# Windowed attention and a gated convolutional feed-forward on one core: batch 0 loaded and attended in two token halves

## The chip, the cores and the metric

The kernel runs on one core of a Trainium2 chip, as one program. The metric is the device time in microseconds (us) of that core. A core has a matrix engine (TensorE, PE in the profile; PEld is its loading of weights), VectorE (DVE), ScalarE (ACT), GpSimd (POOL), and SyncE (SP), whose queue here issues nearly all DMA transfers. The engines run beside each other, each in its own fixed order, and wait for one another through semaphores. PE writes to PSUM, which has eight banks; only DVE and ACT move results from there to SBUF in this kernel.

## The reference: what is computed

There are 8 batches of 576 tokens, 8 heads of 64. Each token attends to the tokens at most 32 places away. The heads are then put side by side (512 numbers per token) and go through a feed-forward with 1024 inner channels and a gate from a convolution over three neighbouring tokens.

```python
scores = scale * np.matmul(q, k.transpose(0, 1, 3, 2))
mask = np.abs(pos[:, None] - pos[None, :]) <= 32
attn = exp(where(mask, scores, -1e9) - max); attn /= attn.sum(-1)
x = np.matmul(attn, v).transpose(0, 2, 1, 3).reshape(B, S, H * D)
h = np.maximum(x @ w_in, 0.0)                      # (B, S, 1024)
conv = sum(conv_w[k] * hp[:, k:k + S, :] for k in range(3))
out = (h * sigmoid(conv)) @ w_out                  # (B, S, 512)
```

## The kernel before

**Attention of one batch.** Heads are taken in four pairs. `loads` (line 349) brings q and k in by four transfers of 576 KB (two for q, two for k: `load_qk`), and v in five blocks of up to 128 tokens (`load_v`); POOL casts each to bf16 (`cast_qk`, `cast_v`). v is cast into `ve`, and DVE copies it shifted by 64 tokens into `vo` (`shift`), so that each window finds its tokens on the right partitions. `transposes` (line 475) turns q and k on PE into `qT` and `kT`, through PSUM and a copy on ACT or DVE. `scores` (line 509) makes the scores of a pair in two pieces (windows 0 to 4 and 5 to 8), ACT takes the exponential into `attn`, and DVE multiplies by the band mask. `values` (line 539) multiplies by v with a column of ones beside it, DVE takes the reciprocal of that sum (`rec`) and scales into `xn`. `x_turned` (line 578) transposes `xn` into `xT`, in groups of two, two and one blocks of 128 tokens.

**Feed-forward.** Two batches are 1152 tokens, cut into three chunks of 384, so there are 12 chunks; chunk 0 lies in batch 0, chunk 1 half in batch 0 and half in batch 1, chunk 2 in batch 1. For a chunk, `first` (line 615) makes eight blocks of 128 inner channels from `w_in_sb` and `xT` (four products each) and a relu on ACT or DVE into `hT`. Chunk 1 is worked in two parts of 193 columns, so that its batch-0 part need not wait for batch 1. `gates` (line 705) does the convolution on PE with 32 x 32 diagonal weights (`diag_w`), four strips of the array at once. A strip's result lands rotated by a multiple of 32 partitions for three of four channel blocks, so `moves` (line 688) copies `hT` rotated into `gT` by DMA; then ACT takes tanh into `tn`, and DVE multiplies (`gT<-tn,hT` for the block that is not rotated, `gT<-tn,gT` for those that were moved). `second` (line 758) multiplies `gT` by `w_out_sb` in three output blocks, which are copied to `wst` and stored.

**Weights.** w_in comes in two halves of 512 columns into the staging tile `ws` (shown as `wst`), cast on POOL (`load_w_in`, line 413); w_out follows into the same tile after batch 1's loads (`load_w_out`, line 429). The stores use that tile, too.

**What sets the order.** No loop of the program order is run as written. Every step is added as a task with the engines that may do it and their assumed durations, its reads and writes, and a target time (`Order.add`, line 39). `Order.run` (line 65) then lists the tasks: of those that are ready on an engine it takes the one with the earliest target, gives out PSUM banks, and where two engines may do a copy takes the one that would end first. The instructions are emitted in the order that comes out and keep it on the chip. The targets come from one table of numbers, `PARAMS` (line 832): the period of the chunks, starts, and an offset for each kind of step. Loads of batch 0 have the target -100, w_in -60, batch 1 -50, w_out -40, so these go in that order on SP. Everything is emitted through one helper, so all rows of the profile name line 274 (line 283 in the changed kernel); steps are told apart by tiles and shapes.

In the shapes, a product of `xT` with `w_in_sb` of 385 or 386 columns is a whole chunk's, one of 193 columns a part of chunk 1. `ident,xn` are the transposes of x; `w_out_sb,gT` with 512 columns the output products.

Of the kernel before, what the change touches and what calls it, by code (L numbers as in the profile page):

```python
# [31 lines left out]
class Order:  # L32
# [3 lines left out]
    def __init__(self):  # L36
        self.tasks, self.writer, self.readers = [], {}, {}

    def add(self, kinds, emit, t, reads=(), writes=(), opens=None, ps=(), after=(), claims=()):


        deps = set(after)
# [10 lines left out]
        task = Task(len(self.tasks), kinds, emit, t, deps, opens, ps)  # L53
        task.soft = soft - deps
        for k in reads:
            self.readers.setdefault(k, []).append(task)
# [138 lines left out]
def kernel(  # L195
# [152 lines left out]

    def loads(b):
        i = b % NLD  # L350

        def load_qk(y, j):
            src = (q, k)[y][b, 4 * j:4 * j + 4, :, :]
            sync.dma_start(
                qkst[y][j].rearrange("p e j d -> p e (j d)"),
                bass.AP(src.tensor, src.offset, [[RP * D, 128], [2 * S * D, 2], [1, RP * D]]),
            )

# [21 lines left out]
        if b < 2:  # L380
            x, dx = (-100.0 if b == 0 else -50.0), 0.1
        else:
            x, dx = t0 - PARAMS["LD"], Q["LX"]
# [5 lines left out]

        for j in range(NPH):  # L390
            for y in range(2):
                t = x + n * dx
                o.add({"SP": dma(256, 110)}, lambda e, y=y, j=j: load_qk(y, j), t,
                      writes=[("st", y, j)], after=paced())
                before.append(o.tasks[-1])
                o.add({"POOL": pl(1152)}, lambda e, y=y, j=j: cast_qk(y, j, e), t,
                      reads=[("st", y, j)], writes=[("b", i, y, j)])
                n += 1
        for c in range(NBLK):
            t = x + n * dx  # L400
            o.add({"SP": dma(1024, 21)}, lambda e, c=c: load_v(c), t, writes=[("vst", c)], after=paced())
            before.append(o.tasks[-1])
            o.add({"POOL": pl(512)}, lambda e, c=c: cast_v(c, e), t,
                  reads=[("vst", c)], writes=[("ve", i, c)])
            n += 1
        for cs in ((0, 2), (2, 4)) if b == 0 else ((0, 4),):
            for half in range(2):
                o.add({"DVE": dve(520 * (cs[1] - cs[0]), 4)},
                      lambda e, cs=cs, half=half: shift(half, cs), x + n * dx,
                      reads=[("ve", i, c + half) for c in range(*cs)],  # L410
                      writes=[("vo", i, c, half) for c in range(*cs)])

    def load_w_in():
        for h in range(2):
# [9 lines left out]
            o.add({"SP": dma(512, 95)}, load, -60.0, writes=[("ws", 4 * h + c) for c in range(4)])  # L424
            for c in range(KC):
                o.add({"POOL": pl(512)}, lambda e, h=h, c=c: cast(e, h, c), -60.0 + h,
                      reads=[("ws", 4 * h + c)], writes=[("w_in", h, c)])

    def load_w_out():
        rows = moe_w_out.rearrange("(h c p) f -> p h c f", c=4, p=128)  # L430
        for c in range(4):
            def load(e, c=c):
                for lo, at, n in turn(c):
# [5 lines left out]
            o.add({"SP": dma(256, 95, len(turn(c)))}, load, -40.0,  # L439
                  writes=[("ws", 4 * h + c) for h in range(2)])  # L440
            for h in range(2):
                o.add({"POOL": pl(512)}, lambda e, h=h, c=c: copy(e, w_out_sb[:, 4 * h + c, :], ws[:, 4 * h + c, :]),
# [18 lines left out]
    def conv_weights():  # L461
        ps = Banks(1)
        o.add({"PE": pe(200.0, "f32")},
              lambda e: tensor.matmul(bank(ps, 0)[:, 0:3 * MB], conv_w24, ident24, start=True, stop=True),
              5.0, opens=ps, writes=[("cw24",)])
        o.add({"DVE": dve(24)}, lambda e: vector.tensor_copy(
            out=conv_w_sb.rearrange("p k m -> p (k m)"), in_=bank(ps, 0)[:, 0:3 * MB]),
            5.0, reads=[("cw24",)], writes=[("cw",)], ps=[ps])
        o.add({"DVE": dve(768)}, lambda e: vector.tensor_tensor(
# [5 lines left out]
    def transposes(g2):  # L475
# [3 lines left out]
        i, n = b % NLD, g2 % NKT  # L479
        for y in range(2):  # L480
# [16 lines left out]
            o.add({"PE": pe(280.0, "rows")}, mm, t + Q["TR"],  # L497
                  reads=[("b", i, y, j)], writes=[("tr", g2, y)], opens=ps,
                  claims=[("T", n, y, h) for h in range(2)])
            for h in range(2):  # L500
                o.add({"ACT": act(576), "DVE": dve(576)},
                      lambda e, ps=ps, h=h, to=to: copy(
                          e, to[:, h, :, :], half(ps, h).rearrange("p (j x) -> p x j", x=64)),
                      t + Q["TC"], reads=[("tr", g2, y)], writes=[("T", n, y, h)], ps=[ps])
# [4 lines left out]
    def scores(g):  # L509
# [3 lines left out]
        for part, ts in enumerate((range(0, 5), range(5, 9))):  # L513
            ps = Banks(2, 2)
            w = 64 * len(ts)

            def mm(e, ps=ps, ts=ts):
                for x in ts:
# [8 lines left out]
            o.add({"PE": pe(28.0 * len(ts), "rows")}, mm, t + Q["SC"] * d,  # L527
                  reads=[("T", n, y_, y) for y_ in range(2)],
                  writes=[("sc", g, part)], opens=ps, claims=[("a", a, part)])
            o.add({"ACT": act(2 * w)},  # L530
# [3 lines left out]
                  t + Q["EX"] * d, reads=[("sc", g, part)], writes=[("a", a, part)], ps=[ps])  # L534
        o.add({"DVE": (850.0, 850.0, None)},
# [3 lines left out]
    def values(g):  # L539
# [5 lines left out]
        ps = Banks(2, 2)  # L545

        def mm(e):
            for h in range(2):
                for c in range(NBLK):
                    for j in range(2):  # L550
                        x = min(2 * c + j, NT - 1)
                        tensor.matmul(
                            bank(ps, h)[64 * j:64 * j + 64, 65 * c:65 * c + 65],
# [6 lines left out]
        o.add({"PE": pe(29.0 * 10, "cols")}, mm, t + Q["AV"] * d,  # L560
              reads=[("a", a, 0), ("a", a, 1)] + [("ve", i, c) for c in range(NBLK)]
              + [("vo", i, c, h) for c in range(NBLK - 1) for h in range(2)],
              writes=[("av", g)], opens=ps, claims=[("xn", b % 2, pr), ("rec", a)])

        def po():
            return pair(ps, 0)[:, :, 0:65 * NBLK].rearrange("p e (c x) -> p e c x", x=65)

        o.add({"DVE": dve(70)}, lambda e: vector.reciprocal(rec, po()[:, :, :, 64]), t + Q["AX"] * d,
              reads=[("av", g)], writes=[("rec", a)], ps=[ps])
        h0 = head(pr, 0)  # L570
        o.add({"DVE": dve(640)},
              lambda e: vector.tensor_tensor(
                  out=xn_pp[b % 2][:, :, h0:h0 + 3:2, :].rearrange("p c e d -> p e c d"),
                  in0=po()[:, :, :, 0:64],
                  in1=rec[:, :, :, None].broadcast_to([128, 2, NBLK, 64]), op=ALU.mult),
              t + Q["AX"] * d, reads=[("av", g), ("rec", a)], writes=[("xn", b % 2, pr)], ps=[ps])

    def x_turned(b, c, n):

        t, d = pair_t[b * NP + NP - 1]  # L580
        t = t + Q["XT"] * d + 0.1 * c
# [7 lines left out]
        def mm(e):  # L589
            for i in range(n):  # L590
# [7 lines left out]
        o.add({"PE": pe(4 * n * (cols / 2.4 + 3))}, mm, t,  # L598
              reads=[("xn", b % 2, i) for i in range(NP)], writes=[("xps", b, c)], opens=ps,
              claims=[("xT", b // 2 % 2, b % 2, c + i) for i in range(n)])  # L600
        o.add({"ACT": act(4 * n * cols), "DVE": dve(4 * n * cols)},
# [4 lines left out]
              writes=[("xT", b // 2 % 2, b % 2, c + i) for i in range(n)], ps=[ps])  # L606


    def span(c, part):
# [3 lines left out]
        return (lo, hi) if part is None else ((lo, lo + HW + 1), (hi - HW - 1, hi))[part]  # L613

    def first(c, m, part, t):
# [19 lines left out]
        def relu(e):  # L635
# [10 lines left out]
            else:  # L646
                o0 = 1 if kind == 0 else 0
# [3 lines left out]
            else:  # L651
# [3 lines left out]
        o.add({"PE": pe(4 * (n / 2.4 + 3))}, mm, t,  # L655
              reads=need + [("w_in", m // 4, i) for i in range(KC)], writes=[("ph", c, m, part)], opens=ps,
              claims=[("h", kind, m, p_) for p_ in ((0, 1) if part is None else (part,))])
        o.add({"ACT": act(n), "DVE": dve(n)}, relu, t + Q["RL"], reads=[("ph", c, m, part)],
              writes=[("h", kind, m, p_) for p_ in ((0, 1) if part is None else (part,))], ps=[ps])
# [28 lines left out]
    def moves(c, qds, part, t):  # L688
        kind, halves, n, taps, gate = views(c, part)
        for s_ in range(1, 4):  # L690
# [10 lines left out]
            o.add({"SP": dma(128 * runs * len(qds), 46 if n > HW and runs == 1 else 28, 2, PARAMS["MV"])},  # L701
# [166 lines left out]
```

## Time and profile before

| | |
|---|---|
| median of 3 runs | 242.4 us (242.24 to 243.18) |
| the profiled execution | 243.37 us |
| its span, first to last instruction | 241.7 us |
| busy: PE, DVE, ACT, POOL | 208.1, 160.1, 164.0, 80.9 us |
| weight loads (PEld) | 124.3 us |
| DMA, mean rate over the span | 205 GB/s, 49.62 MB |
| mean granted PE clock | 0.972 |

A row of the profile in order of time gives the start, the length, the engine, the line, the operation, the written and the read tile, their shapes and a count; in brackets stands the idle time of that engine just before, and what ended it. A row of a stretch gives, for a window of the span, how long each engine was busy in it, the clock that PE was granted (1.00 is full speed), and the share of the 16 DMA engines that was in use. A row of a group gives the busy time of all its instructions, the mean length of one in ns, and the idle time before them.

### The profile page before, as it was taken

The page shows a single profiled execution, that of the slowest core. Times are in us where ns is not written, and L with a number is a line of the kernel's source. Part 1 is how long each engine was busy: PE and PEld are TensorE (multiplying, and loading weights), DVE is VectorE, ACT ScalarE, POOL GpSimd, SP SyncE. Part 2 cuts the span into 40 slices and gives each one's busy share as a digit, 9 for nine tenths or more (in the row PEclk, how much of TensorE's full clock was granted, in tenths as well). Part 3 has the DMA queues.
Part 4 walks back from the last instruction along what each step waited for, and adds up shares of the span by engine and source line. Part 5 has one row for each costly group of instructions (what it writes and reads, how often), then busy time and mean ns, then how long its engine had stood idle before and what let it go on. Part 6 is the DMA issues. An engine that isn't in the chain of part 4 may idle for free. (4 is left out here: it accounts for less than half of the span.)

```text
span 241.7 us, 9128 instructions
## 1 busy us (share of the span) xinstructions
PE 208.1 (86%) x3878; PEld 124.3 (51%) x3906; DVE 160.1 (66%) x268; ACT 164.0 (68%) x291; POOL 80.9 (33%) x96
## 2 busy tenths in 40 slices
PE   1536995589998869999999998999999999999993
PEld 0425464365655454565455654655555655555541
DVE  7586166998575899546399779698684595524140
ACT  1650586445698576679977886679778885876751
POOL 5757744536613444662236517321000000000000
PEclk9999999758999997999999999999999999999999
DMA  6999999989698899969489989756132223342534
GB/s 237 292 289 392 248 233 223 275 229 337 168 290 186 217 293 355 328 186 278 98 207 356 264 225 281 161 129 205 37 129 55 79 105 68 123 110 54 177 113 181
DMA packets 67228, 49.62 MB, mean 205 GB/s; under 512 B 46172, under 2 KB 52340, under 8 KB 67188
## 3 DMA queue, kind: packets, MB, share of 16 engines
q1 hardware_dynamic: 67152, 49.03, 71.6%
q8 instruction: 30, 0.49, 0.9%
q14 instruction: 10, 0.08, 0.1%
q10 hardware_dynamic: 36, 0.01, 0.0%
HBM read 32.52 MB, written 9.44 MB: 174 GB/s over the span
## 5 line engine op out<-in xcount | busy, mean ns | idle before, releaser
L274 PE MATMUL pst<-xT,w_in_sb 128*128 128x385 bf16 (+2 forms) x416 | 75.4, 322 | 1.6 <-ACT xT L274 0.6
L274 PE MATMUL pst<-w_out_sb,gT 128*128 128x512 bf16 x260 | 64.3, 384 | 3.2 <-issue 2.2
L274 PEld LDWEIGHTS <-w_in_sb 128*128 128x128 bf16 x416 | 37.6, 100 | 25.8 <-issue 3.4
L274 ACT ACTIVATE hT<-pst 128x385 bf16<-128x385 f32 (+2 forms) x80 | 38.6, 489 | 11.1 <-PE pst L274 10.1
L274 DVE SCALAR_TENSOR_TENSOR gT<-tn,gT 128x384 bf16<-128x384 f32 (+2 forms) x52 | 42.4, 842 | 3.9 <-DMA gT<-hT 3.9
L274 POOL CAST ve<-vst 128x512 bf16<-128x512 f32 x40 | 29.4, 741 | 45.7 <-DMA vst<-in_v_dram 43.5
L274 ACT ACTIVATE attn<-pst 128x640 bf16<-128x640 f32 x64 | 39.4, 667 | 4.9 <-PE pst L274 4.9
L274 PEld LDWEIGHTS <-gT 128*128 128x128 bf16 x288 | 26.6, 99 | 31.0 <-issue 3.3
L274 ACT ACTIVATE tn<-pst 128x768 f32<-128x768 f32 (+1 forms) x52 | 37.4, 768 | 6.5 <-PE pst L274 4.6
L274 ACT COPY wst<-pst 128x512 f32<-128x512 f32 x36 | 21.2, 588 | 29.6 <-PE pst L274 28.1
L274 DVE TENSOR_TENSOR attn<-attn,mask 128x1152 bf16<-128x1152 bf16 x32 | 26.9, 846 | 12.3 <-ACT attn L274 12.1
L274 DVE TENSOR_TENSOR xn<-pst,rec 128x640 bf16<-128x640 f32 x32 | 25.8, 818 | 0.5
L274 DVE SCALAR_TENSOR_TENSOR gT<-tn,hT 128x384 bf16<-128x384 f32 (+1 forms) x26 | 14.7, 564 | 16.5 <-ACT tn L274 16.4
L274 POOL CAST qb<-qst 128x1152 bf16<-128x1152 f32 x16 | 19.9, 1242 | 16.2 <-DMA qst<-in_q_dram 12.5
L274 POOL CAST kb<-kst 128x1152 bf16<-128x1152 f32 x16 | 19.9, 1243 | 16.0 <-DMA kst<-in_k_dram 14.3
L274 PE MATMUL pst<-hT,diag_w 32*32 32x384 bf16 (+1 forms) x1248 | 21.2, 322 | 1.8 <-DVE xn L274 1.0
L274 ACT COPY xT<-pst 128x1024 bf16<-128x1024 bf16 (+1 forms) x16 | 11.8, 781 | 13.9 <-PE pst L274 13.9
L274 PEld LDWEIGHTS <-attn 128*64 128x64 bf16 x640 | 14.1, 119 | 13.6 <-issue 8.6
L274 PE MATMUL pst<-ve,attn 128*64 128x65 bf16 x384 | 17.4, 206 | 3.8 <-DVE attn L274 2.3
L274 PE MATMUL pst<-qT,kT 64*128 64x64 bf16 x576 | 17.5, 197 | 3.1 <-DVE kT L274 0.8
L274 PE MATMUL pst<-vo,attn 128*64 128x65 bf16 x256 | 15.6, 206 | 3.3 <-DVE vo L274 3.3
L274 PEld LDWEIGHTS <-kT 64*128 64x128 bf16 x576 | 12.2, 98 | 12.0 <-issue 9.2
(37 smaller groups left out, 163.4 us busy)
## 6 DMA issues: line engine op xcount, KB each, us to landing
qst<-in_q_dram SPq DMA_DIRECT2D x16, 576.0 KB, 6.4
kst<-in_k_dram SPq DMA_DIRECT2D x16, 576.0 KB, 7.3
out_dram<-wst SPq DMA_DIRECT2D x11, 768.0 KB, 5.8
vst<-in_v_dram SPq DMA_DIRECT2D x24, 256.0 KB, 5.5
vst<-in_v_dram SPq DMA_DIRECT2D x16, 192.0 KB, 5.9
wst<-in_moe_w_in_dram SPq DMA_DIRECT2D x2, 1024.0 KB, 7.9
gT<-hT SPq DMA_DIRECT2D x14, 144.0 KB, 3.6
gT<-hT SPq DMA_DIRECT2D x34, 48.0 KB, 2.1
```

The lines of the kernel that those rows point to most:

```text
L274: return lambda *args, **kwargs: fixed(do(*args, **kwargs))
```

## The change

*Batch 0 in two halves.* q and k of batch 0 are loaded in eight transfers instead of four: `load_half` takes 288 of the 576 tokens of four heads, 32 groups of nine tokens per head on 128 partitions. Casts (`cast_half`) and transposes (`transposes_half`, 64 x 64 tiles, one PSUM bank for both sides of the pair) follow per half. The scores of batch 0's pairs are split into windows 0 to 3 and 4 to 8; the first piece needs the first half alone. Mask, values, reciprocal and scaling are done per part: blocks 0 and 1, then blocks 2 to 4. The first transposed group of x (blocks 0 and 1) needs the first part only.

*w_in between them.* Half of w_in is loaded behind the first half of batch 0, the other half behind the second; its casts may go to POOL or ACT.

*Chunk 0 in two parts.* Its `first` is done for columns 0 to 192 (193 columns) and 193 to 384 (192), each with relus of its own; convolution, moves and gates are of the whole chunk as before.

*First transfers in a fixed order.* The loads of batch 0, w_in, batch 1 and w_out form a chain (`lead`): each is listed only after the one before it.

*Targets set anew.* `PARAMS` has other numbers, and a table `NUDGE` adds to the target of each kind of step a number of its own for each batch or chunk (and part). The copy of `xT` is assumed twice as fast on DVE as it was.

```diff
-    def add(self, kinds, emit, t, reads=(), writes=(), opens=None, ps=(), after=(), claims=()):
+    def add(self, name, kinds, emit, t, reads=(), writes=(), opens=None, ps=(), after=(), claims=(), sub=0, line=None):
+        index = self.index + 20 * sub
+        t += self.nudge.get(name, {}).get(index, 0.0)
...
+        if line:
+            soft.add(line[-1])
+        if line is not None:
+            line.append(task)
...
+        def load_half(y, j, half):
+            src = (q, k)[y][b, 4 * j:4 * j + 4, 32 * RP * half:32 * RP * half + 32 * RP, :]
+            sync.dma_start(
+                qkst[y][j][:, half, :, :].rearrange("p j d -> p (j d)"),
+                bass.AP(src.tensor, src.offset, [[S * D, 4], [RP * D, 32], [1, RP * D]]),
+            )
...
+        if b == 0:
+            for half in range(2):
+                t = x + 3.0 * half
+                for j in range(NPH):
+                    for y in range(2):
+                        o.add("qk", {"SP": dma(128, 110)}, lambda e, ...: load_half(y, j, half), ..., line=lead)
+                        o.add("qc", {"POOL": pl(576)}, lambda e, ...: cast_half(y, j, half, e), ...)
+                for c in (range(0, 3), range(3, NBLK))[half]:
+                    v_block(c, t)
+                v_shift((2 * half, 2 * half + 2), t)
+                load_w_in(half, t + 1.0)
+            return
...
-                o.add({"POOL": pl(512)}, lambda e, h=h, c=c: cast(e, h, c), -60.0 + h,
+                o.add("wic", {"POOL": pl(512), "ACT": act(512)}, lambda e, h=h, c=c: cast(e, h, c), t,
...
+        def mm(e):
+            for x in range(RP):
+                for h in range(2):
+                    rows = slice(64 * h, 64 * h + 64)
+                    tensor.transpose(turned()[rows, x, :], half_of(y, j, half)[rows, x, :], ident[rows, rows])
...
-        for part, ts in enumerate((range(0, 5), range(5, 9))):
+        for part, ts in enumerate((range(0, 4), range(4, 9)) if first_ else (range(0, 5), range(5, 9))):
...
+        cs = range(NBLK) if part is None else (range(0, 2), range(2, NBLK))[part]
...
-        o.add({"ACT": act(4 * n * cols), "DVE": dve(4 * n * cols)},
+        o.add("xc", {"ACT": act(4 * n * cols), "DVE": dve(4 * n * cols, 2)},
...
+        if c == 0:
+            for m in range(MB):
+                first(c, m, 0, T0 + Q["A0"] + m * 0.5)
...
-PARAMS = {"P": 23.98, "T0": 17.65, "T1": 35.65, "T2": 7.73, "B1": 27.27, "LD": 15, "LEAD": 0, ...
+PARAMS = {"P": 26.5, "T0": 10, "T1": 34.66, "T2": 16, "B1": 22.98, "LD": 21.05, "LEAD": 6.54, ...
+NUDGE = {
+    "qk": {0: 52.49, 1: -11.43, 2: 14.07, ...},
...
```

More of the change, by code (lines that the diff above doesn't have):

```diff
@@ L346 @@
         start[c] = T1 + PARAMS["T2"] + (c - 2) * PC
+    lead = []
     def loads(b):
@@ L525, in mm @@
                         )
[L527 to L530, printed above, removed]
+            o.add("sc", {"PE": pe(28.0 * len(ts), "rows")}, mm, t + Q["SC"] * d,
+                  reads=need, writes=[("sc", g, part)], opens=ps, claims=into,
+                  sub=part if first_ else 0)
+            o.add("ex", {"ACT": act(2 * w)},
                   lambda e, ps=ps, ts=ts, w=w: scalar.activation(
@@ L744, in product @@
                         scalar=1.0, in1=gate(m) if m0 else taps(m, 1), op0=ALU.add, op1=ALU.mult)
-            o.add({"DVE": dve(n * count)}, product, late,
+            o.add("pr", {"DVE": dve(n * count)}, product, late,
                   reads=[("tn", tn_i, u) for u in us] + ii,
-                  writes=[("g", c % 3, m + x, p_) for x in range(count) for p_ in halves])
+                  writes=[("g", c % 3, m + x, p_) for x in range(count) for p_ in halves],
+                  sub=qd + 2 * int(c == 1 and part == 0))
     tn_count = [0]
```

223 lines of the change are left out of this document (149 added, 74 removed), and 73 rows, old and new, of tables (NUDGE, PARAMS).

## The prediction

> **What bounds the kernel now.** I read the stretches first, then the order of time of the first 60 us, then the groups by form and the waits of TensorE. The stretches:
>
> ```profile
> 0.00:42.00 42.00, 24.66 (x514) 17.75 (x514) 25.51 (x57) 20.52 (x35) 25.62 (x38) 1.00 1.01 274
> 42.00:60.00 18.00, 14.05 (x301) 9.55 (x302) 16.80 (x29) 8.73 (x17) 9.53 (x10) 0.72 0.93 278
> 60.00:80.00 20.00, 18.51 (x440) 11.40 (x442) 13.38 (x22) 17.21 (x34) 8.20 (x10) 1.00 0.86 221
> 80.00:100.00 20.00, 16.83 (x276) 10.29 (x275) 16.71 (x24) 12.79 (x23) 10.34 (x10) 0.91 0.99 298
> 102.00:238.00 136.00, 132.06 (x2298) 74.09 (x2318) 86.40 (x137) 102.89 (x183) 26.03 (x28) 1.00 0.56 160
> ```
>
> The columns of the stretches are length, then busy PE, weight loads, DVE, ACT, POOL, then granted clock, DMA share and GB/s. From 102 us on PE is the bound: busy 132.06 of 136, so 3.9 us are all that an order can win there. The idle time lies ahead of that: 17.3 us in 0 to 42, 4.0 in 42 to 60 (with the clock at 0.72), 1.5 in 60 to 80, 3.2 in 80 to 100. In the same stretches the DMA share is about 1.0, and DVE is busy 16.80 of 18 and 16.71 of 20.
>
> The order of time in the first 60 us (start, length, engine, what) shows when each load is in and what waits for it:
>
> ```profile
> 4.76 1.14 POOL L274 CAST qb<-qst 128x1152 bf16<-128x1152 f32 x1 [1.65 <-DMA qst<-in_q_dram]
> 10.15 1.15 POOL L274 CAST kb<-kst 128x1152 bf16<-128x1152 f32 x1 [0.78 <-DMA kst<-in_k_dram]
> 16.49 0.99 POOL L274 CAST ve<-vst 128x512 bf16<-128x512 f32 x1 [0.56 <-DMA vst<-in_v_dram]
> 21.63 2.29 POOL L274 CAST w_in_sb<-wst 128x512 bf16<-128x512 f32 x4 [0.44 <-DMA wst<-in_moe_w_in_dram]
> 34.57 0.62 POOL L274 CAST ve<-vst 128x512 bf16<-128x512 f32 x1 [1.53 <-DMA vst<-in_v_dram]
> ...
> 22.99 2.00 PE L274 MATMUL pst<-ident,xn 128*128 128x128 bf16 x18 [1.07 <-DVE xn L274]
> 25.54 4.12 PE L274 MATMUL pst<-xT,w_in_sb 128*128 128x385 bf16 x16 [0.55 <-ACT xT L274]
> 39.36 0.85 PE L274 MATMUL pst<-xT,w_in_sb 128*128 128x193 bf16 x8
> 52.46 1.48 PE L274 MATMUL pst<-xT,w_in_sb 128*128 128x193 bf16 x8
> 58.23 1.89 PE L274 MATMUL pst<-w_out_sb,gT 128*128 128x512 bf16 x7
> 48.90 0.82 DVE L274 TENSOR_TENSOR xn<-pst,rec 128x640 bf16<-128x640 f32 x1
> 49.64 3.70 DVE L274 SCALAR_TENSOR_TENSOR gT<-tn,gT 128x384 bf16<-128x384 f32 x4
> ```
>
> Batch 0 is wholly in at 16.5 us, w_in at 21.6, batch 1 at 34.6 (each number is the start of the cast that waited). The first feed-forward product starts at 25.54. Batch 1's attention then runs through DVE until 49.7, and the first product that needs batch 1 is the one at 52.46. So there are two starts to watch: 25.54 and 52.46.
>
> **The change, part by part.**
>
> *Loads in halves.* Bytes and packets of q and k stay the same (one row of 576 numbers each); four transfers become eight. Four whole ones come in (10.15 - 4.76) / 3 = 1.8 us apart, so a half takes 0.9. The new queue is q/k first half, three v blocks, half of w_in, then the same again, then batch 1, then w_out. A v block takes (16.49 - 10.15) / 5 = 1.27 us, half of w_in (21.63 - 16.49) / 2 = 2.6. That puts the first q/k half in at 6.6, its v at 10.4, half of w_in at 13.0, the second q/k half at 16.6, its v at 19.1, the rest of w_in at 21.7. Batch 1 follows at the same times as before, since nothing was taken out ahead of it. The condition is that the queue never runs dry; a share of 1.01 says it has work queued throughout.
>
> [...]
>
> *First half of batch 0.* Four copies, four exponentials, masks, values, scaling and two transposition blocks follow each other mostly on ACT and DVE. A row in order of time, and groups by form (busy, mean ns, idle before):
>
> ```profile
> 5.07 1.28 ACT L274 ACT_TABLE_LOAD   x1 [5.07 <-DVE conv_w_sb L274]
> ...
> L274 ACT ACTIVATE attn<-pst 128x512 bf16<-128x512 f32 x32 | 19.6, 613 | 0.8 <-PE pst L274 0.8
> L274 ACT ACTIVATE attn<-pst 128x640 bf16<-128x640 f32 x32 | 23.1, 721 | 4.1 <-PE pst L274 4.1
> L274 ACT COPY qT<-pst 128x576 bf16<-128x576 bf16 x23 | 14.2, 647 | 0.3 <-PE pst L274 0.3
> L274 DVE TENSOR_TENSOR attn<-attn,mask 128x1152 bf16<-128x1152 bf16 x32 | 26.9, 846 | 12.3 <-ACT attn L274 12.1
> L274 DVE RECIPROCAL rec<-pst 128x10 f32<-128x10 f32 x32 | 6.5, 211 | 11.8 <-PE pst L274 10.0 <-ACT hT L274 1.4
> L274 DVE TENSOR_TENSOR xn<-pst,rec 128x640 bf16<-128x640 f32 x32 | 25.8, 818 | 0.5
> L274 DVE COPY xT<-pst 128x1024 bf16<-128x1024 bf16 x6 | 4.1, 691 | 7.8 <-PE pst L274 7.7
> L274 ACT COPY xT<-pst 128x1024 bf16<-128x1024 bf16 x10 | 10.1, 1017 | 13.7 <-PE pst L274 13.7
> ```
>
> ACT is free at 6.35 and all four copies stand on it: 4 x 0.65 + 4 x 0.61 ends at 11.4. Then the last mask (512 of 1152 columns of 0.85: 0.4), values (an estimate of 0.5), four reciprocals of 0.21 and four scalings of two fifths of 0.82 (2.2 together), 8 of the 18 transposing products of the row at 22.99 (0.9) and the copy (0.7) make 16.1. So 16 narrow products (193 columns) start 9.4 us sooner. At 0.85 per eight (the row at 39.36) they and the next 16, which wait for the second half of w_in, are 3.4 us of PE work taken out of the stretch after 25.54.
>
> The second half ends no sooner: its v lands at 19.1 where the whole had landed at 16.5, and its transpositions stand in PE's order behind the 16 products. From 17.8 (16.1 and two times 0.85) on come two copies (1.3), four exponentials of 0.72 (2.9), a mask (0.5), values (0.5 again), a reciprocal and three fifths of a scaling (0.7), 12 of 18 transposing products (1.3) and two copies (0.9 by columns): 25.9, against the 25.54 of before. This costs nothing by itself, as PE then has only 64 narrow products left (6.8 us) and must wait for batch 1's v at 34.6 either way.
>
> *Batch 1.* Here the end of the head is set. In the new order of DVE two shifts of v, then keys, then three scalings come; before the last scaling stand four gate products of chunk 0, and behind it six gate products of chunk 1 and only then the two copies of the transposed x, all on DVE. The gate products wait for the moved rows (issues in order of time, then the moves' landing in 30 to 60, then the products' group):
>
> ```profile
> 34.58 8.04 SPq L274 DMA_DIRECT2D gT<-hT  x6
> 44.51 4.12 SPq L274 DMA_DIRECT2D gT<-hT  x6
> ...
> DMA to landing us min/median/max: 4.4/6.1/9.5
> ...
> L274 DVE SCALAR_TENSOR_TENSOR gT<-tn,gT 128x384 bf16<-128x384 f32 x26 | 16.2, 634 | 0.0
> ```
>
> The last row of the moves of chunk 0 is issued at 42.6 and in at 48.7; those of chunk 1 are issued until 48.6 and in at 54.7 by the median. So the last scaling ends near 51.8 (before: 49.72), the gate products of chunk 1 near 55.4 (54.7 and one of 0.63), the first copy at 56.1, and the product that needs batch 1 starts at 56.2 instead of 52.46: 3.7 later. But by then PE has behind it both conv groups of chunk 1's first part and two of the three output groups of chunk 0, which before ran only until 60.12, less the 16 narrow products (1.7) that before had done by then. So 56.2 in the new kernel stands for 60.1 - 1.7 = 58.4 in the old: a gain of 2.2. The end of the move is the uncertain term: at 4.4 or 9.5 instead of 6.1 the gain is 3.9 or -1.2.
>
> [...]
>
> *Batch 2.* The next hold of before:
>
> ```profile
> 80.33 0.94 POOL L274 CAST ve<-vst 128x512 bf16<-128x512 f32 x1 [1.26 <-DMA vst<-in_v_dram]
> 83.23 0.19 PE L274 MATMUL pst<-vo,attn 128*64 128x65 bf16 x1 [0.73 <-DVE vo L274]
> 86.58 1.78 DVE L274 SCALAR_TENSOR_TENSOR gT<-tn,gT 128x768 bf16<-128x768 f32 x1
> 89.15 0.44 PE L274 MATMUL pst<-ident,qb 64*128 64x64 bf16 x18 [0.78 <-DVE xn L274]
> ```
>
> Its last v block is cast at 80.33, and a gate product of 1.78 stands before the last scaling. In the new order that product stands behind the x copies (a shorter one of 0.63 is in its place), and the last v block of batch 2 is issued ahead of chunk 2's moves instead of behind the first of them. I take 1.2 (1.78 - 0.63), and of the 1.8 that the clock costs there (0.09 x 20) another 0.4, my choice for what follows from a shorter wait: a gain of 1.6. For the 2.2 of the head to last, v must land 2.2 sooner; the DMA share of 0.86 in 60 to 80 leaves 2.8 us of room.
>
> *The rest.* Ten 256-column copies of x move from ACT to DVE: 10 x 0.69 = 6.9 us more on DVE, 10 x 1.02 = 10.2 less on ACT, both beside PE. 32 more narrow products and their weight loads add under 0.3. Four casts of w_in go from POOL to ACT, which had idle time there. The new targets reorder everything; from 102 us on they can win at most 3.9. What they can lose has no row of its own; the nearest is the largest wait of PE between 102 and 238:
>
> ```profile
> PE pst L274 <- DVE xn L274: 1.0, 1, 1.0
> ```
>
> I take a loss of 1.0, since DVE has more to do per batch and PE had almost no idle time to lose. The end is alike: output products of chunk 11, a copy, a store.
>
> *Sum.* The profiled execution took 243.37 (span 241.7, 1.67 around it), 0.97 above the median of 242.4. 243.37 - 2.2 - 1.6 + 1.0 = 240.6; at the median's level 239.6.
>
> **The rivals.**
>
> *Slower: DVE's queue.* DVE runs in order, so a late move holds the copies of x behind the gate products of chunk 1. If the last move lands after 9.5 us, the product of 56.2 starts at 59.6, 1.2 behind before, and from a landing past 56.9 the head is lost. With the batch-2 gain gone too and the 1.0 of the rest kept, this is 243.37 + 1.2 + 1.0 = 245.6, at the median's level 244.6. For it: DMA share 0.93 in that stretch, more DVE work. Against it: the median of 6.1.
>
> *No change: the loads are the bound.* To 100 us the DMA share is 0.86 or more, and all bytes stay. If batch 2's v comes no sooner than 80.33, the head's 2.2 turns into waiting there, and with 1.6 - 1.0 left the time is 241.8. For it: the cast that waited at 80.33; against it: the room of 2.8 us and the issue order.
>
> *Halved loads arrive late.* If four extra transfers each exposed the 0.9 us that a half takes, everything of batch 1 comes 3.6 later: 239.6 + 3.6 = 243.2. Against it are the 1.8 us between whole transfers. [...]
>
> *More than I count.* If the new targets also win half of the 3.9 after 102 us in place of the 1.0 lost, 236.7.
>
> **How the numbers follow.** A measurement here tells about 0.5% (1.2 us) from no change. Forecast 0.48 (own range 238 to 241), more 0.12, loads bound 0.16, DVE's queue 0.18, late halves 0.06. All of the first two are faster: 0.60; the loads case lies within 0.5%, 0.15 of it counted as same and the rest as slower; slower 0.25. The range leaves out 1 in 10 on each side: from 235.5 (the move at 4.4 and the gain in the rest) to 244.6.
>
> **What would show it.** Right: a narrow product near 16; the first product on batch 1 near 56 with two output groups of chunk 0 ahead of it; no 768-column gate product between scalings of batch 2; PE idle in 80 to 100 below 3.2. Wrong: that start past 58.4, a dry DMA queue before 42, or more than 5 us of PE idle after 102.

## The result, and the profile after

The changed kernel took 262.31 us (median of 4 runs, 260.81 to 263.44). Its ratio to the kernel before is 1.0808, 95% interval 1.0725 to 1.0892: 19.6 us slower, where 2.8 us faster was forecast. The profiled execution took 263.1 us (span 261.4, granted clock 0.926 against 0.972). Some kernels below scatter by a few per cent from run to run; ratios are taken over their undisturbed runs, where there were enough of these, and the profiled executions with one head per transfer, with whole loads (the first run), with pairs of heads and with rows in line are among the longer ones of their kernels.

The stretches of the changed kernel, with the columns as in the prediction (the last one is the same distance from the end as the last one of before):

```profile
0.00:42.00 42.00, 17.85 (x338) 14.14 (x339) 16.11 (x54) 14.17 (x25) 15.03 (x27) 0.88 0.56 182
42.00:60.00 18.00, 11.77 (x270) 10.09 (x268) 6.55 (x12) 12.55 (x26) 10.48 (x14) 0.88 1.07 233
60.00:80.00 20.00, 15.74 (x297) 10.59 (x298) 17.02 (x27) 6.93 (x14) 10.04 (x10) 0.60 0.89 283
80.00:100.00 20.00, 18.77 (x415) 11.23 (x414) 12.58 (x22) 16.30 (x34) 7.35 (x9) 1.00 0.76 194
121.70:257.70 136.00, 133.69 (x2261) 73.75 (x2253) 90.39 (x144) 95.09 (x169) 24.06 (x28) 0.99 0.58 157
```

The loss lies ahead of the last 136 us, in the head: in those 136 us PE idles 2.3 us (before: 3.9). In 0 to 42 PE idles 24.2 us instead of 17.3, and the DMA share has fallen from 1.01 to 0.56, though the same bytes are wanted at the same time. From 60 to 80 PE has a clock of 0.60 and idles 4.3 us (before: 1.00 and 1.5).

The order of time of the changed kernel, POOL's casts and some PE rows:

```profile
6.79 0.66 POOL L283 CAST qb<-qst 128x576 bf16<-128x576 f32 x1 [3.67 <-DMA qst<-in_q_dram]
16.23 0.72 POOL L283 CAST kb<-kst 128x576 bf16<-128x576 f32 x1 [2.19 <-DMA kst<-in_k_dram]
21.93 1.18 POOL L283 CAST w_in_sb<-wst 128x512 bf16<-128x512 f32 x2 [2.75 <-DMA wst<-in_moe_w_in_dram]
33.70 0.67 POOL L283 CAST kb<-kst 128x576 bf16<-128x576 f32 x1 [2.46 <-DMA kst<-in_k_dram]
50.86 0.62 POOL L283 CAST ve<-vst 128x512 bf16<-128x512 f32 x1 [0.41 <-DMA vst<-in_v_dram]
...
25.69 2.67 PE L283 MATMUL pst<-xT,w_in_sb 128*128 128x193 bf16 x16
60.00 0.50 PE L283 MATMUL pst<-ident,kb 64*128 64x64 bf16 x12 [4.29 <-issue]
78.49 2.16 PE L283 MATMUL pst<-xT,w_in_sb 128*128 128x193 bf16 x24
```

The four first halves of q and k come in from 6.79 to 16.23, (16.23 - 6.79) / 3 = 3.15 us apart; the forecast had 0.9. Batch 1's last v is cast at 50.86 instead of 34.57. The first narrow product runs at 25.69 (forecast 16.1), the first that needs batch 1 at 78.49 (forecast 56.2, before 52.46).

The DMA view of the changed kernel from 0 to 40 us, in 40 slices of 1 us (tenths of the 16 DMA engines in use, then GB/s):

```profile
DMA  0022222742249223979983223932224735999899
GB/s 0 12 35 62 85 101 104 212 109 99 104 153 222 96 101 94 238 123 299 408 331 124 101 104 126 240 96 101 101 101 145 189 109 124 356 379 333 312 403 399
```

The same view of the kernel before from 0 to 14 us, in slices of 0.35 us:

```profile
DMA  0000048999999999899999999999999999999999
GB/s 0 0 0 0 0 90 314 382 349 303 356 382 408 408 375 316 303 382 408 402 402 402 395 339 298 274 208 220 218 219 217 219 215 218 219 212 233 223 176 97
```

While half loads are under way, the share stands at 2 tenths and the rate near 101 GB/s. Before, the share was 8 or 9 tenths as soon as the first load had begun, and the rate 303 to 408 GB/s from 2.1 to 8.0 us. So the queue was not dry: it moved its transfers at a lower rate.

### The profile page after: what moved, and what is told of

It reads as the page before. It is cut to its first block, busy times and chain, and to the rows that moved or that the text cites. A ratio compares the mean times of both kernels' runs of the same rounds, so it can differ in the third digit from the quotient of the medians.

```text
span 261.4 us, 9383 instructions
## 1 busy us (share of the span) xinstructions
PE 216.9 (83%) x4010; PEld 132.5 (51%) x4010; DVE 162.1 (62%) x287; ACT 161.3 (62%) x296; POOL 79.0 (30%) x96
## 4 chain that ended last, share of the span: by engine, by line
PE 68%; DVE 8%; SPq 7%; DMA 6%; ACT 5%; issue 5%; POOL 0%; ACTq 0%; DVEq 0%
PE pst L283 68%; SPq L283 7%; DMA kst<-in_k_dram 6%; ACT attn L283 3%; DVE gT L283 2%; DVE attn L283 2%; ACT tn L283 1%; DVE xn L283 1%; DVE vo L283 1%; DVE kT L283 1%; DVE hT L283 1%; ACT kT L283 0%; ACT hT L283 0%; DVE rec L283 0%; DVE xT L283 0%
## 5 line engine op out<-in xcount | busy, mean ns | idle before, releaser
L283 PE MATMUL pst<-xT,w_in_sb 128*128 128x385 bf16 (+3 forms) x448 | 74.4, 315 | 3.1 <-issue 2.3
L283 ACT ACTIVATE hT<-pst 128x385 bf16<-128x385 f32 (+3 forms) x90 | 40.3, 463 | 13.8 <-PE pst L283 13.0
L283 ACT ACTIVATE attn<-pst 128x640 bf16<-128x640 f32 (+1 forms) x64 | 38.8, 661 | 6.1 <-PE pst L283 5.6
L283 DVE TENSOR_TENSOR attn<-attn,mask 128x1152 bf16<-128x1152 bf16 (+2 forms) x36 | 27.3, 767 | 17.8 <-ACT attn L283 17.4
L283 POOL CAST qb<-qst 128x1152 bf16<-128x1152 f32 (+1 forms) x18 | 20.4, 1133 | 29.0 <-DMA qst<-in_q_dram 23.1
L283 POOL CAST kb<-kst 128x1152 bf16<-128x1152 f32 (+1 forms) x18 | 19.8, 1101 | 29.5 <-DMA kst<-in_k_dram 27.3
L283 DVE TENSOR_TENSOR xn<-pst,rec 128x640 bf16<-128x640 f32 (+2 forms) x36 | 26.1, 739 | 0.5
L283 DVE TENSOR_SCALAR hT<-pst 128x385 bf16<-128x385 f32 (+3 forms) x22 | 10.4, 478 | 21.7 <-PE pst L283 16.1
L283 ACT COPY qT<-pst 128x576 bf16<-128x576 bf16 x23 | 14.5, 651 | 13.9 <-PE pst L283 13.9
L283 DVE SCALAR_TENSOR_TENSOR gT<-tn,hT 128x384 bf16<-128x384 f32 (+1 forms) x26 | 14.3, 554 | 11.9 <-ACT tn L283 11.9
L283 ACT COPY kT<-pst 128x576 bf16<-128x576 bf16 x20 | 12.9, 656 | 10.3 <-PE pst L283 10.2
```

The source lines that it names most:

```text
L283: return lambda *args, **kwargs: fixed(do(*args, **kwargs))
```

## The experiments

**Theory A.** A half load's source has the four heads outermost (4 x 32 rows), the whole load's is one run of 128 rows. A transfer with 4 outermost uses a quarter of the DMA engines, and that is all that is wrong. **Rivals.** Not the pattern but the new order or the new targets (B, D); or any pattern that isn't a plain run of rows is slow, whatever its outermost count (C). In the expectations on record the letters shift. In the first four, up to that with 16 x 8 rows, B is a fixed cost that each transfer pays one after another, and C the new targets and the split feed-forward. Further on B is what else the new order changed, C a pattern that isn't a plain run of rows, and D the new targets and the fixed order. The text uses the later letters.

**One head per transfer.** Each half load as four transfers of 32 rows, the order otherwise as it was:

```diff
-                bass.AP(src.tensor, src.offset, [[S * D, 4], [RP * D, 32], [1, RP * D]]),
+            for hd in range(4):  # to partitions 32 * hd ...
+                    bass.AP(src.tensor, src.offset + hd * S * D, [[RP * D, 32], [1, RP * D]]),
```

> The changed kernel, with each half load of q or k written as four transfers of one head (32 rows of 2304 B, outermost count 32) instead of one whose source has 4 heads outermost; the planner's task and so the order of everything else stay. Theory A (a transfer uses only as many of the 16 DMA engines as its outermost count allows, here 4, so a half load takes 3.3 us where 0.9 was forecast, and everything behind it in the queue slips): the DMA share in 6 to 18 rises from 0.40 and 0.60 to above 0.8, issue (0.5 us each) becomes the limit, the first half of q and k is in by 10 instead of 16.2, batch 1's last v cast comes near 40 instead of 50.9, and the time falls by 8 to 15 us, to 247 to 254. Theory B (small transfers each pay a fixed cost in series): four times as many transfers make it slower than 262. Theory C (the new targets and the split feed-forward are what costs): 262 within 3 us even if the loads come sooner.

Measured: 254.34 us, ratio 1.0454 (1.0344 to 1.0564). Rows of SP's queue and of PE:

```profile
0.80 1.80 SPq L283 DMA_DIRECT2D qst<-in_q_dram  x4
12.95 6.08 SPq L283 DMA_DIRECT2D kst<-in_k_dram  x4
...
70.67 2.16 PE L283 MATMUL pst<-xT,w_in_sb 128*128 128x193 bf16 x24
```

A third to a half of the loss goes, though there are four times as many transfers, so a fixed cost per transfer, which would have made it slower, falls. The time is just above the 247 to 254 of theory A. Each transfer costs SP 0.45 us to issue (1.80 for four), and the issues stall (6.08 for four), so the loads are still late (batch 1's last v is cast at 43.6) and this says little about the rest.

**Halves taken out.** The changed kernel with q and k of batch 0 loaded, cast and transposed whole; values, scalings and chunk 0 stay in parts, and targets and order of loads stay.

```diff
-                for j in range(NPH):
+                for j in range(NPH if half == 0 else 0):
...
-lambda e, y=y, j=j, half=half: load_half(y, j, half)
+lambda e, y=y, j=j: load_qk(y, j)
```

> The changed kernel with q and k of batch 0 loaded, cast and transposed whole, as before; v, w_in, chunk 0, attention pieces, chain and new targets stay. Theory A: batch 1 is in at 35 again, and the time is 240 to 245, near before. Theory B: the same. Theory C: still above 255, since the targets stay.

Measured: 244.71 us (240.28 to 246.0, 4 runs). Run again for an interval:

> The changed kernel with q and k of batch 0 loaded, cast and transposed whole, as in the earlier run of it, for an interval: what the new targets, the values and scalings in parts and chunk 0 in two parts cost without halves. If they win what the prediction gave them (3.8 less 1.0): 238 to 241. If they cost: 243 to 246, ratio 1.005 to 1.015.

Measured: 245.41 us, ratio 1.0056 (1.0003 to 1.011). The second run's PE had these rows:

```profile
43.46 0.44 PE L283 MATMUL pst<-ident,qb 64*128 64x64 bf16 x18
...
62.87 2.16 PE L283 MATMUL pst<-xT,w_in_sb 128*128 128x193 bf16 x24
```

So without half loads some 18 of the 19.6 us are gone, but what is left wins nothing: it costs about 1.4 us by this ratio (0.1 to 2.7 by its interval). The prediction gave all parts together 3.8 less 1.0; the 2.2 of that for the head was reckoned with half loads.

**The pattern alone, in the kernel before.** Two runs wrote batch 0's whole loads as 4 x 32 rows (the edit below) and as 16 x 8 rows.

```diff
-[[RP * D, 128], [2 * S * D, 2], [1, RP * D]]
+[[32 * RP * D, 4], [RP * D, 32], [2 * S * D, 2], [1, RP * D]]
```

> The kernel before, with only the source of batch 0's four q and k loads written as 4 x 32 rows instead of 128: same bytes, same number of transfers, same rows of 2304 B. Theory A: a transfer of 576 KB takes 6.6 us (four engines) instead of 1.8, the four are in near 29 instead of 10.2, and the time rises by 15 to 20 us, to 257 to 263. Theories B and C: 242 to 243, as nothing but the writing of the pattern changes.

> The same as the one with 4 x 32, but 16 x 8 rows. Theory A: all 16 engines again, 242 to 244, the fourth cast near 10.2. If it is the extra dimension of the pattern that costs, and not its outermost count: as slow as with 4 x 32.

Measured: ratio 0.9991 (0.9911 to 1.0071), and 242.28 us. They don't decide. Such rows follow each other evenly, and that the two dimensions were merged into the one run of 128 again is the author's estimate: the trace doesn't show the source's pattern, but with 4 x 32 the four casts start at 4.77 to 11.29 (before: 4.76 to 10.15), and in both runs the semaphore of a load goes up in sixteen separate steps, as before. What is needed is a pattern whose blocks don't follow each other evenly. In the next three runs each of batch 0's four q and k tiles comes by two transfers of 288 KB, as in the changed kernel, with n = 4, 8 or 16 outermost:

```diff
+            if b == 0:
+                for e in range(2):
+                    sync.dma_start(
+                        qkst[y][j][:, e, :, :].rearrange("p j d -> p (j d)"),
+                        bass.AP(src.tensor, src.offset + 128 // n * RP * D * e,
+                                [[256 // n * RP * D, n], [RP * D, 128 // n], [1, RP * D]]))
+                return
```

> The kernel before, in which each of batch 0's four q and k tiles is loaded by two transfers of 288 KB whose source pattern is that of the changed kernel's half loads: 4 outermost, 32 groups, 576 elements. Bytes and rows (2,304 B) are those of before; batch 0's rows land on other partitions, so its output is not the reference's. Theory A (a transfer whose outermost count is 4 uses 4 of the 16 DMA engines): each transfer takes about 3.3 us, as the half loads of the changed kernel did, eight of them 26 us, so the last cast of batch 0's k is at about 29 instead of 11, batch 1's last v about 15 to 18 later, and the time 254 to 264 us. Rival B (the half loads were slow because of what else changed in the new order, not by their pattern): each takes 0.9 us, the time stays at 240 to 246.

> The same kernel with the same eight transfers of 288 KB, the source written as 8 outermost, 16 rows, 576 elements; batch 0's rows land on other partitions, so its output is not the reference's. Theory A (as many engines as the outermost count): 1.65 us each, eight of them 13 us instead of 7, the last k cast at about 17, the time 244 to 250 us. Rival C (a pattern that can't be merged, or a third dimension, is slow whatever its count): as with 4 outermost, 3.3 us each and the same time as that run.

> The same kernel with the same eight transfers of 288 KB, the source written as 16 outermost, 8 rows, 576 elements; batch 0's rows land on other partitions, so its output is not the reference's. Theory A: all 16 engines, 0.9 us each, the last k cast within 2 us of before (11.3), the time 240 to 246 us. Rival C (not the count, but that the pattern has a third dimension): 3.3 us each and 254 to 264 us, as with 4 outermost.

Measured: ratios 1.0683 (1.0595 to 1.0771), 1.025 (1.0191 to 1.0309) and 1.0117 (1.0056 to 1.0179). First and last q and k cast of batch 0 and the DMA share (40 slices of 5 to 35, 4 to 14 and 3 to 10 us), for 4 outermost, then 8, then 16:

```profile
9.55 1.14 POOL L274 CAST qb<-qst 128x1152 bf16<-128x1152 f32 x1 [6.44 <-DMA qst<-in_q_dram]
27.61 1.15 POOL L274 CAST kb<-kst 128x1152 bf16<-128x1152 f32 x1 [4.86 <-DMA kst<-in_k_dram]
DMA  2222222222222239222222224932239999869999
```

```profile
7.15 1.14 POOL L274 CAST qb<-qst 128x1152 bf16<-128x1152 f32 x1 [4.04 <-DMA qst<-in_q_dram]
16.94 1.46 POOL L274 CAST kb<-kst 128x1152 bf16<-128x1152 f32 x1 [1.79 <-DMA kst<-in_k_dram]
DMA  5555464455545555579986544544554545789996
```

```profile
5.91 1.14 POOL L274 CAST qb<-qst 128x1152 bf16<-128x1152 f32 x1 [2.79 <-DMA qst<-in_q_dram]
12.51 1.15 POOL L274 CAST kb<-kst 128x1152 bf16<-128x1152 f32 x1 [0.95 <-DMA kst<-in_k_dram]
DMA  8997999999999999979979989999999999989999
```

A tile is two transfers, so a transfer takes (27.61 - 9.55) / 6 = 3.0 us, 1.6 and 1.1, at shares of 2, 5 and 9 tenths. Between the three only the outermost count changed, and with it the rows in a run. The first load's semaphore goes with it: beside one step at the issue, it goes up in four steps as the data lands with 4 outermost (6.18 to 6.56 us) and in the changed kernel (6.47 to 6.74), in eight with 8; with 16 outermost, and before, there are sixteen steps and none at the issue. As far as these three counts go, theory A stands (which of the 16 engines carried a transfer no view shows), and rivals B and C for the load fall. With 16 outermost the kernel is still 1.2% behind: eight transfers at 1.1 are slower than four at 1.8. Whether that is the price of the split or of this pattern was not parted.

**Pairs of heads.** Each half load as two transfers of two heads, written 32 x 2 with the heads interleaved on the partitions, and put right where the transposes are copied out of PSUM:

```diff
+            for h in range(2):  # to partitions 64 * h ...
+                    bass.AP(src.tensor, src.offset + 2 * h * S * D, [[RP * D, 32], [S * D, 2], [1, RP * D]]),
...
-turned().rearrange("p j (y x) -> p y x j", y=2)
+turned().rearrange("p j (x y) -> p y x j", y=2)
```

> The changed kernel, each half load made as two transfers of two heads each (32 outermost, 2 heads, 576 elements, 144 KB), the two heads interleaved on the partitions and put right in the eviction of the transposes; order and targets as they are. Theory A (the outermost count was the only fault): the first q and k half in at 7 to 8 us, the narrow FFN products start at 17 to 20 instead of 25.7, batch 1's last v in at 35 to 38 instead of 50.9, and the time 238 to 247 us. Rival D (the new targets and the split of chunk 0 cost most of the 20 us): above 250 us with the loads on time. If the mended loads beat the kernel before, the forecast's other steps held; if it ends within 1% of it, they cancel.

Measured: 251.67 us (245.49 to 253.07, 6 runs; the profiled execution took 252.34).

```profile
38.07 1.22 POOL L283 CAST ve<-vst 128x512 bf16<-128x512 f32 x2 [0.48 <-DMA vst<-in_v_dram]
...
69.02 2.16 PE L283 MATMUL pst<-xT,w_in_sb 128*128 128x193 bf16 x24
```

From 10 to 20 us the DMA share is 0.94 (changed kernel: 0.63). Batch 1 is in by 38.7 us, 4 us behind before, but the first product on it is 16.6 behind, 1.9 of it by a longer stall of PE ("issue", 4.12 for 2.17, see the last section). So in this execution theory A is not the whole, and rival D may have a part. The times don't decide it: 245.49 lies in the range of theory A, the median in that of D.

**The loads just as forecast.** To settle that, the changed kernel with each half load taking 128 consecutive rows, instead of 32 of each of four heads, in one transfer of the same size; batch 0's output is then not the reference's:

```diff
-[[S * D, 4], [RP * D, 32], [1, RP * D]]
+[[RP * D, 128], [1, RP * D]]
```

> The changed kernel, in which each half load takes 128 consecutive rows of q or k (one transfer of 288 KB, 128 outermost) instead of 32 rows of each of four heads. Bytes, transfers, casts, transposes and every engine's order are those of the changed kernel; the rows of batch 0's q and k are the wrong ones, so its output for batch 0 is not the reference's. This gives the prediction the loads that it reckoned with. Theory A (the half loads were the only fault): w_in's halves are cast from about 13 and 22, the narrow FFN products start at 16 to 18, batch 1's last v is cast by 35 to 37, and the time is 236 to 243 us. Rival D (the fixed order and the targets cost as well, as the run with paired heads hints at): with the loads as forecast the time is still 245 to 252, batch 1's second pair of transposes runs after 42 (before: 36.4), and the granted clock stays under 0.96.

Measured: 249.23 us (244.59 to 252.16, 6 runs), ratio 1.016 (1.0075 to 1.0245). The profiled execution took 251.32. Its order of time on POOL and PE, then on DVE:

```profile
12.96 1.17 POOL L283 CAST w_in_sb<-wst 128x512 bf16<-128x512 f32 x2 [1.98 <-DMA wst<-in_moe_w_in_dram]
22.06 1.43 POOL L283 CAST w_in_sb<-wst 128x512 bf16<-128x512 f32 x2 [1.88 <-DMA wst<-in_moe_w_in_dram]
34.63 0.62 POOL L283 CAST ve<-vst 128x512 bf16<-128x512 f32 x1 [1.50 <-DMA vst<-in_v_dram]
...
16.75 2.75 PE L283 MATMUL pst<-xT,w_in_sb 128*128 128x193 bf16 x16 [0.16 <-DVE xT L283]
30.93 1.06 PE L283 MATMUL pst<-ident,xn 128*128 128x128 bf16 x8
40.18 1.37 PE L283 MATMUL pst<-hT,diag_w 32*32 32x384 bf16 x96
43.34 0.44 PE L283 MATMUL pst<-ident,qb 64*128 64x64 bf16 x18
46.42 0.50 PE L283 MATMUL pst<-ident,kb 64*128 64x64 bf16 x12 [2.22 <-issue]
60.28 3.57 PE L283 MATMUL pst<-w_out_sb,gT 128*128 128x512 bf16 x8 [0.34 <-DMA kst<-in_k_dram]
65.34 1.89 PE L283 MATMUL pst<-w_out_sb,gT 128*128 128x512 bf16 x8
67.07 2.16 PE L283 MATMUL pst<-xT,w_in_sb 128*128 128x193 bf16 x24
...
23.80 3.10 DVE L283 TENSOR_TENSOR attn<-attn,mask 128x640 bf16<-128x640 bf16 x3
32.02 0.69 DVE L283 COPY xT<-pst 128x1024 bf16<-128x1024 bf16 x1 [1.97 <-PE pst L283]
49.21 3.31 DVE L283 TENSOR_TENSOR attn<-attn,mask 128x1152 bf16<-128x1152 bf16 x2
54.19 1.96 DVE L283 SCALAR_TENSOR_TENSOR gT<-tn,gT 128x384 bf16<-128x384 f32 x2
56.88 2.61 DVE L283 SCALAR_TENSOR_TENSOR gT<-tn,gT 128x768 bf16<-128x768 f32 x2
59.41 0.81 DVE L283 TENSOR_TENSOR xn<-pst,rec 128x640 bf16<-128x640 f32 x1
```

Before, batch 1's second transposes started with this row:

```profile
36.38 0.44 PE L274 MATMUL pst<-ident,qb 64*128 64x64 bf16 x18
```

The loads are on the forecast to 0.4 us (12.96, 22.06 and 34.63 for 13.0, 21.7 and 34.6), and the first narrow product is at 16.75 for 16.1. From there on it goes another way. Batch 0's last x is transposed at 30.93 and its copy ends at 32.7 instead of 25.9; batch 1's second transposes run at 43.34 instead of before's 36.38; its last scaling starts at 59.41, behind gate products of chunk 0; and the first product on it is at 67.07 instead of 56.2.

**A later target.** The same kernel with the target of chunk 0's first part 16 us later (`"A0": -4.0` to `12.0`), by which PE takes batch 1's second transposes before half of chunk 0's convolution.

> The same kernel, and the target of chunk 0's first part moved 16 us later (A0 from -4 to 12), by which the list puts batch 1's second transposes and two pairs of its scores ahead of half of chunk 0's convolution instead of behind all of it. Theory A: no difference beyond 1 us. Rival D, in the form that PE's fixed order holds batch 1's attention back: batch 1's second transposes run 2 to 4 us sooner and the time falls by 1 to 4 us against the run with rows in line.

Measured: 258.38 us, ratio 1.0727 (1.0636 to 1.0818).

```profile
39.45 0.43 PE L283 MATMUL pst<-ident,qb 64*128 64x64 bf16 x18
63.77 2.16 PE L283 MATMUL pst<-xT,w_in_sb 128*128 128x193 bf16 x24
```

Rival D's local claim holds: 3.9 us sooner there, 3.3 sooner at the first product on batch 1. But the time is 9 us worse, which neither theory expected. The one number changed the list of the whole kernel, and PE loses more later than was won: from 70 to 170 us it idles 11.9 us, with rows in line 6.0. The run says that the order of the list matters; it can't say what the earlier attention alone is worth.

**DVE's queue.** The kernel with rows in line again, with the four gate products of chunk 0 that stand ahead of batch 1's last scalings cut to 8 columns, and no order changed:

```diff
+                if c == 0 and m0:
+                    vector.scalar_tensor_tensor(
+                        out=gate(m)[:, 0:1, 0:8], in0=tn[:, m0, 0:8].rearrange("p (i x) -> p i x", x=8),
+                        scalar=1.0, in1=gate(m)[:, 0:1, 0:8], op0=ALU.add, op1=ALU.mult)
```

> The kernel with rows in line, in which the four gate products of chunk 0 that stand between batch 1's last two scalings on DVE (1.96 + 2.61 us in that run) work on 8 of their columns; chunk 0's output is not the reference's, nor batch 0's. The orders stay. If DVE's queue sets the end of batch 1's attention there: its last scaling starts at 54 to 56 instead of 59.4, the first product that needs batch 1 at 61 to 64 instead of 67.1, and the time falls by 3 to 4.5 us, to 244.5 to 246.5. If PE and its clock set it: the same starts within 1 us and a time of 248 to 250.

Measured: 245.59 us, ratio 1.0092 (1.0045 to 1.0138).

```profile
44.62 0.35 PE L283 MATMUL pst<-ident,kb 64*128 64x64 bf16 x12 [0.76 <-issue]
51.33 0.23 DVE L283 SCALAR_TENSOR_TENSOR gT<-tn,gT 128x8 bf16<-128x8 f32 x2
52.80 0.23 DVE L283 SCALAR_TENSOR_TENSOR gT<-tn,gT 128x8 bf16<-128x8 f32 x2
52.95 0.82 DVE L283 TENSOR_TENSOR xn<-pst,rec 128x640 bf16<-128x640 f32 x1
61.49 2.16 PE L283 MATMUL pst<-xT,w_in_sb 128*128 128x193 bf16 x24
```

The last scaling starts 6.5 us sooner: 4.1 by the products (2.61 and 1.96 against twice 0.23), 1.5 by a shorter stall of PE's issue (0.76 for 2.22), which the edit didn't aim at, the rest mostly by shorter masks. From its first mask at 47 to 49 us on, DVE waits no longer than 0.4 us at a time in either run, so its queue does set the end of batch 1's attention. The medians fall by 3.6; the ratios by 0.7 points, with overlapping intervals, so in the time itself the effect is not parted from the scatter.

## Why the prediction was wrong

**The step that failed is *Loads in halves*: "so a half takes 0.9".** It read 1.8 us from whole transfers and halved it, since bytes and rows stayed; its condition, a queue that never runs dry, was met, and the time was lost inside the transfers: 3.15 us each, 2.25 more than the forecast for each of eight, 18 us by that sum. Batch 1's last v was 16.3 us late. The share of 1.01 in the trace was that of the loads of before, whose q and k have 128 rows outermost, and the diff showed another pattern, with 4. The rival *halved loads arrive late* (0.06) had the direction, by another mechanism and at 0.9 instead of 2.25 a piece. By the ratios, giving the loads their forecast times takes 6.5 of the 8.1 points away, some 16 of 19.6 us.

**A second step was wrong as well: *First half of batch 0*, "25.9 ... This costs nothing by itself".** With the loads as forecast the second half ended at 32.7. The 16 products ran at 172 ns instead of 107 (2.75 for 1.7), and behind the exponentials the forecast had one mask, one reciprocal and three fifths of a scaling; three masks (3.10), four reciprocals and four scalings came in a row on DVE until 29.4. Why the products were slower stays open. And the idle PE time that was to absorb it was not idle: the remaining products and chunk 0's convolution (40.18) stand ahead of batch 1's second transposes in PE's fixed order, which came at 43.34. With whole loads these came at 43.46, behind the same convolution and a stall of 2.48, so this belongs to the new order and not to the halves.

**Batch 1: the place was right, the sizes not.** The step named DVE's queue, gate products of chunk 0 before the last scaling and x copies behind those of chunk 1, and that is what the trace shows; the forecast rival *DVE's queue* put 1.2 us on it through late moves. It was a late start: the last scaling ended at 60.2 for 51.8, a figure for which the prediction shows no sum. Its conversion (56.2 in the new kernel is as far as 58.4 in the old) held roughly. The table sets the start of the first product on batch 1, less 58.4, beside the profiled execution's excess over 243.37; each line is one execution:

| kernel | start | less 58.4 | excess |
|---|---|---|---|
| changed | 78.49 | 20.1 | 19.7 |
| one head per transfer | 70.67 | 12.3 | 12.0 |
| pairs of heads | 69.02 | 10.6 | 9.0 |
| rows in line | 67.07 | 8.7 | 7.95 |
| light gate products | 61.49 | 3.1 | 1.3 |
| whole loads, first run | 61.61 | 3.2 | 1.2 |
| whole loads, second run | 62.87 | 4.5 | 0.45 |
| later target | 63.77 | 5.4 | 15.0 |

Apart from the last, whose later order differs, all do better than the conversion, by 0.3 to 2.0 us and once by 4.0. A gain behind the start would look like this, and the prediction had given 1.6 to *Batch 2*, whose scalings do stand ahead of the 768-column product in the changed kernel; but no run took that alone, and with this scatter the table doesn't show it.

**The clock.** Of the gain of 1.6 in batch 2 the prediction put 0.4 on the clock; no run shows this term, as none changed the clock alone; in 80 to 100 the changed kernel had 1.00 instead of 0.91, but ran some 20 us behind by then. What the traces show is a lower clock in the head: 0.60 was granted in 60 to 80 of the changed kernel (before: 1.00), and with rows in line half the clock from 44.3 to 64.7 (before: 45.4 to 55.6). There eight output products took 3.57 us at 60.28, at half the clock, and 1.89 at 65.34, past it. What lowered the clock was not shown.

**The rest.** From 102 us on PE lost no 1.0 but idled 1.6 us less. What stays open: with loads on time and light gate products the kernel is still 0.9% behind, and with whole loads 0.6%. Late batch 0, the stall of PE's issue and the clock may share it; they were not parted. No version of the changed kernel here beat the kernel before. One sum of the prediction is off by its own terms, with nothing resting on it: the lower end of its range, the move at 4.4 and the gain in the rest, comes to 236.7 - 1.7 = 235.0 and not 235.5.

## What to carry to other kernels

Here a DMA's time followed its pattern, not its bytes alone. So before halving a transfer, look which count is outermost (the runs here varied it in the source): 288 KB took 3.0 to 3.15 us with 4, 1.6 with 8, 1.1 with 16, and 0.8 to 1.1 with 128 in one run. A cut by tokens across heads put a 4 there; put the long count outermost, even if the data then lands interleaved (with 32 the DMA share was 0.94 in 10 to 20 us, with 4 0.63). And when a step is split, count its work on each queue once per piece, and look what stands in front of the next consumer in the fixed orders: slack on an engine is none where its order puts other work first.

## What the runs showed of the hardware

*Issue.* SP needs 0.45 us per transfer (1.80 for four, with one head per transfer), and eight transfers of 288 KB with 16 outermost took 1.1 us each where four of 576 KB took 1.8 before; as one run of 128 rows the first four halves were cast 1.1 us apart and the second four 0.8.

*PE's stall.* PE stood still for "issue" where no operand was missing: 4.29 us in the changed kernel, 2.22 and 0.76 above. Counted in the trace of PE's instructions, weight loads and semaphore instructions included, 961 or 1217 of them, 256 apart, stand ahead of the place in all 14 traces, while the length goes from 0.33 to 4.29 us and differs between executions of one program (1.46 and 2.48 in the two runs with whole loads). Before, the row was this:

```profile
39.22 0.21 PE L274 MATMUL pst<-ident,kb 64*128 64x64 bf16 x2 [2.17 <-issue]
```

In all 14 traces the stall ended 1.3 to 1.6 us after a packet of 16 KB had landed on the queue that the profile marks "instruction" (at 58.55 in the changed kernel, at 37.86 before). That PE waited for its code here is the author's estimate from these counts and landings. The DMA share was 0.98 and 1.02 in these two stalls; whether the loads made them longer, no run tested.

*DVE beside POOL.* The same three masks of 640 columns that took 3.10 us with rows in line, while POOL was casting batch 1's q and k, took 1.30 in the changed kernel, where POOL waited for loads until 38.29:

```profile
37.41 1.30 DVE L283 TENSOR_TENSOR attn<-attn,mask 128x640 bf16<-128x640 bf16 x3
```

That POOL's casts are the cause was not tried by a run of its own. If they are, the late loads hid a cost that timely ones brought out.
